# The first row tile's normalization ahead of the second's statistics, and the last row tile's two column halves in two PSUM banks

## Chip, cores and metric

One core of a Trainium2 chip. The metric is the device time of one launch in microseconds (us). A run's span, which the profile shows, is 1.7 to 1.9 us shorter than its time. All runs counted were at a granted TensorE clock of 0.999 to 1.0. All times inside a profile are us from the start of the span.

## The reference

A transformer block in bf16 on 2048 rows of 1024: layer norm, dilated local attention (32 heads, window 8, dilation 2), residual; layer norm, a bilinear gated feed-forward of width 3584, residual.

```python
x = A_x                                                    # (1, 2048, 1024)
h = x + _A_ref(_layernorm(x), A_wqkv, A_wo)                # qkv product, attention, product with wo
h2 = h + _B_ref(_layernorm(h), B_w_gate, B_w_up, B_w_down) # ((h @ w_gate) * (h @ w_up)) @ w_down
```

## The kernel before

The rows are worked on in four chunks of 512, each of four row tiles of 128. Products run on TensorE into eight PSUM banks (`psum`, 128 x 512 fp32 each). The order of instructions on each engine is the order of the program (`manual_schedule`).

**The start.** The first chunk is normalized tile by tile: statistics on VectorE, `Ln` and `Exp` on ScalarE for the scale, the normalization on VectorE in two halves, eight transposes on TensorE, two copies on ScalarE, and 32 small matmuls with weight block 0, of which eight `ko` slices are loaded in two transfers.

```python
    load_w0(0, 4)                       # ScalarE's DMA queue, 512 KB each
    load_w0(4, 4)
    for t in range(4):
        load_x0(t)                      # SyncE's DMA queue, 256 KB each
    nc.scalar.preload_act_table_set("natural_log_exp_and_others")
    # ... (cut: warm-up matmuls, constants)
    first_half(0, 0)                    # statistics of one half of a row tile
    first_half(0, 1)
    first_rstd(0)                       # aggregate (VectorE), Ln and Exp (ScalarE)
    for t in range(4):
        if t < 3:
            first_half(t + 1, 0)
        first_norm(t)
        if t < 3:
            first_half(t + 1, 1)
        if t > 0:
            first_mm(t - 1, range(0, 6))
        first_transpose(t)              # TensorE transposes, ScalarE copies
        if t > 0:
            first_mm(t - 1, range(6, 8))
        if t < 3:
            first_rstd(t + 1)
    first_mm(3, range(8))
```

**The middle.** While TensorE multiplies, a list of background work (`bg`) is dealt out between the matmul groups: statistics of later chunks, attention on VectorE. ScalarE both takes the `Ln` and `Exp` of these statistics and casts finished PSUM banks into SBUF (`evac_qkv`, tile `sg`), in program order. Near 510 us VectorE builds sums of activations and of weights for the feed-forward of the last two chunks.

```python
    xtiles[3] = load_x(3, "x", nc.sync)
    pump(6)
    bg.add(stats_gen(norm1[3]), bg.now + 6.0)     # ready 6.0 later on the kernel's own schedule
    # ... (cut)
    activation_sums(l2, l3, dn["px"])             # VectorE, needs the transposed rows l2 and l3
    weight_sums(0, nc.vector)                     # VectorE, needs weights only
```

**The end.** The last product adds 14 slices to each of four row tiles; their sums stand in the banks `ps_y[0..3]`. The fourth tile is done as two column halves of one bank, so that the last read and store are short.

```python
    def dprod(ps, q, lhs, rhs, fresh, lo=0, n=TC):
        for k in range(NP):             # NP = 14
            nc.tensor.matmul(ps[:, bass.ds(lo, n)], lhsT=lhs[k][:, bass.ts(q, 128)], rhs=rhs[k][:, bass.ds(lo, n)], ...)
    # result(): VectorE reads ps[:, lo:lo+n], scales and adds, then SyncE stores the rows
    for q, lo, n in ((0, 0, 512), (1, 0, 512), (2, 0, 512), (3, 0, 256), (3, 256, 256)):
        dprod(ps_y[q], q, HF["12"], fcells(down["b22"]), False, lo, n)
        result(2, hs2[q], q, 1, ps_y[q], inv, p5[q], lo, n)
```

Of the kernel before, what the change touches and what calls it, by code (L numbers as in the profile page):

```python
# [78 lines left out]
def kernel(  # L79
# [11 lines left out]
    nc = tc.nc  # L91
# [180 lines left out]
    def load_x0(t):  # L272
        nc.sync.dma_start(x0[t][:], x[bass.ds(t * 128, 128), :])

    def load_w0(lo, n):
        nc.scalar.dma_start(w0[:, lo:lo + n, :], wqkv_v[:, lo:lo + n, 0:512])

    load_w0(0, 4)
    load_w0(4, 4)
    for t in range(4):  # L280
        load_x0(t)
    nc.scalar.preload_act_table_set("natural_log_exp_and_others")
    warm = t1k.tile([128, TC], BF, tag="t1k", name="warm")
    nc.vector.memset(warm[:], 0.0)
    eps = const.tile([128, 1], F32)
# [39 lines left out]
    def first_half(t, i):  # L325
        if i == 0:
            sts[t] = small.tile([128, 2, nc.vector.BN_STATS_DIM], F32, tag="st", name=f"st0_{t}")
        nc.vector.bn_stats(out=sts[t][:, i, :], in_=x0[t][:, bass.ts(i, 512)])

    def first_rstd(t):  # L330
        nc.vector.bn_aggr(out=mv0[:, t, :], in_=sts[t][:])
        rstd_of(mv0, rs0, t, t + 1)
# [3 lines left out]
    def first_norm(t):  # L336
        lns[t] = lnp.tile([128, D], BF, tag="ln", name=f"ln0_{t}")
        for i in range(2):
            cols = bass.ts(i, 512)
            nc.vector.tensor_scalar(lns[t][:, cols], x0[t][:, cols], mv0[:, t, 0:1], rs0[:, t:t + 1],  # L340
                                    ALU.subtract, ALU.mult)

    def first_transpose(t):
        for hf in range(2):
            pt = psum.tile([128, KO // 2, 128], BF, tag="mm", name=f"pt{t}_{hf}")
            for kk in range(KO // 2):
                nc.tensor.transpose(pt[:, kk, :], lns[t][:, bass.ts(4 * hf + kk, 128)], ident[:])
            nc.scalar.copy(lnTs[0][:, bass.ts(hf, 4), bass.ts(t, 128)], pt[:])

    def first_mm(t, kos):  # L350
        for ko in kos:
            for j in range(4):
                nc.tensor.matmul(ps0[j][:, bass.ts(t, 128)], lhsT=wts["qkv", 0][:, ko, bass.ts(j, 128)],  # L353
                                 rhs=lnTs[0][:, ko, bass.ts(t, 128)], start=(ko == 0), stop=(ko == KO - 1))
# [3 lines left out]
    first_half(0, 1)  # L358
    first_rstd(0)
    for t in range(4):  # L360
        if t < 3:
            first_half(t + 1, 0)
        first_norm(t)
        if t < 3:
            first_half(t + 1, 1)
        if t > 0:
            first_mm(t - 1, range(0, 6))
        first_transpose(t)
# [4 lines that stand above are left out]
# [386 lines left out]
    def f16(ap):  # L759
        return ap.bitcast(F16)  # L760
# [19 lines left out]
    def fcells(homes):  # L780
        return [f16(t[:, k, :]) for t in homes for k in range(NH)]

    def dprod(ps, q, lhs, rhs, fresh, lo=0, n=TC):
        for k in range(NP):
            nc.tensor.matmul(ps[:, bass.ds(lo, n)], lhsT=lhs[k][:, bass.ts(q, 128)], rhs=rhs[k][:, bass.ds(lo, n)],  # L785
                             start=(fresh and k == 0), stop=(k == NP - 1), skip_group_check=not fresh)

    def result(c, rows, t, hf, ps, sc, other, lo=0, n=TC):
        cols = bass.ds(hf * 512 + lo, n)
        nc.vector.scalar_tensor_tensor(rows[:, cols], ps[:, bass.ds(lo, n)], sc,  # L790
                                       rows[:, cols] if other is None else other[:, bass.ds(lo, n)], ALU.mult, ALU.add)
        nc.sync.dma_start(outf[bass.ds(c * TC + t * 128, 128), cols], rows[:, cols])
# [124 lines left out]
    hs2 = hss[2]  # L917
# [83 lines left out]
    down = {}  # L1001
# [28 lines left out]
    ps_x = [psum.tile([128, TC], F32, tag="mm", name=f"dx{q}") for q in range(4)]  # L1030
    ps_y = [psum.tile([128, TC], F32, tag="mm", name=f"dy{q}") for q in range(4)]
# [6 lines left out]
    for q in range(4):  # L1038
        dprod(ps_x[q], q, HA["11"], fcells(down["b11"]), True)
        if q == 1:  # L1040
            scale_h.total(ps_y[3])
            inv = const.tile([128, 1], F32, name="inv_hd")
            nc.vector.tensor_tensor(inv[:], scale_h.inv, scale_d.inv, ALU.mult)
            inv = inv[:]
# [3 lines left out]
    HF = {k: [f16(a) for a in HA[k]] for k in HA}  # L1048
# [17 lines left out]
    p5 = []  # L1066
# [21 lines left out]
    for q in range(4):  # L1088
        dprod(ps_x[q], q, HF["22"], fcells(down["b21"]), False)
        result(3, hs3[q], q, 0, ps_x[q], inv, None)  # L1090
    for q, lo, n in ((0, 0, 512), (1, 0, 512), (2, 0, 512), (3, 0, 256), (3, 256, 256)):
        dprod(ps_y[q], q, HF["12"], fcells(down["b22"]), False, lo, n)
        result(2, hs2[q], q, 1, ps_y[q], inv, p5[q], lo, n)


# [1 line left out]
_INS = ['A_x', 'A_wqkv', 'A_wo', 'B_x', 'B_w_gate', 'B_w_up', 'B_w_down']  # L1097
# [26 lines left out]
```

## Time and profile before

| | before |
|---|---|
| time, median of 5 runs (range) | 780.2 us (779.79 to 780.25) |
| span of the profiled run | 778.0 us |
| TensorE busy | 770.7 us, 99% |
| first statistics of row tile 0 | 3.76 |
| first 128x512 matmul of the stage after the start | 17.12 |
| first matmul of the last row tile to the end of the span | 7.35 us |

The prediction quotes the lines of this profile. In a timeline line the columns are start, duration, engine, source line, operation, output and input tiles, shapes, count, and in brackets the idle time of the engine before it with what ended it. Neighbours of one kind are merged into one line ("x24").

### The profile page before, as it was taken

To read this page: it belongs to the slowest core of one execution; us is meant where nothing else is said; L and a number is where in the kernel's file an instruction comes from. 1 tells how busy PE (TensorE), PEld (TensorE's weight loads), DVE (VectorE), ACT (ScalarE), POOL (GpSimd) and SP (SyncE) were. 2 spreads that over 40 slices of the span, in tenths; PEclk is the share of its full clock that TensorE was granted. 3 is DMA by queue.
4 is the path that set the end of the run, shared out by engine and by line. 5 is a ranking of instruction groups with operands and counts; after the bars stand their busy time and mean duration, and the time that the engine had idled before them with its cause. 6 is when DMAs were issued, how large, how long until landed. Compare 5 with 4: busy or idle time off the path is not lost.

```text
span 778.0 us, 10494 instructions
## 1 busy us (share of the span) xinstructions
PE 770.7 (99%) x3707; PEld 355.2 (46%) x3707; DVE 614.8 (79%) x805; ACT 473.3 (61%) x1028; POOL 142.1 (18%) x152
## 2 busy tenths in 40 slices
PE   8999999999999999999999999999999999999997
PEld 6544444444444444444444444444444444444444
DVE  6619999999899998999989989985554444579762
ACT  4626544323576652966769799746777677788230
POOL 0000000010000200002000001008778677600000
PEclk9999999999999999999999999999999999999999
DMA  8999693895955869867645383734332323730001
GB/s 279 254 230 209 166 286 84 259 297 144 341 191 169 298 206 237 276 208 247 219 155 196 115 308 107 168 91 115 101 106 58 109 72 92 260 119 28 1 27 55
DMA packets 181605, 133.86 MB, mean 172 GB/s; under 512 B 79024, under 2 KB 174384, under 8 KB 179504
## 3 DMA queue, kind: packets, MB, share of 16 engines
q1 hardware_dynamic: 176912, 110.12, 49.6%
q0 software_dynamic: 3584, 22.02, 8.2%
q10 hardware_dynamic: 1056, 1.05, 0.4%
q8 instruction: 29, 0.48, 0.3%
q14 instruction: 24, 0.20, 0.1%
HBM read 104.86 MB, written 22.02 MB: 163 GB/s over the span
## 4 chain that ended last, share of the span: by engine, by line
PE 89%; DVE 9%; DMA 1%; issue 0%; ACT 0%; SPq 0%; DVEq 0%
PE ps L390 20%; PE pu L390 12%; PE pg L390 12%; PE dx L785 6%; PE pz L678 6%; PE acc L624 6%; PE py L678 6%; PE px L678 6%; PE wo L511 4%; PE pv L678 3%; PE dy L785 3%; DVE h L832 1%; PE ps L353 1%; PE ex L785 1%; DVE h L790 1%; DVE prodx L778 1%
## 5 line engine op out<-in xcount | busy, mean ns | idle before, releaser
L390 PE MATMUL ps<-lnT,w_qkv 128*128 128x512 bf16 x736 | 159.7, 379 | 0.0
L390 PEld LDWEIGHTS <-w_qkv 128*128 128x128 bf16 x736 | 71.8, 98 | 85.9
L390 PE MATMUL pg<-lnT,w_wg 128*128 128x512 bf16 x448 | 105.8, 379 | 0.0
L390 PE MATMUL pu<-lnT,w_wu 128*128 128x512 bf16 x448 | 105.8, 379 | 0.0
L304 ACT CAST sg<-ps 128x512 bf16<-128x512 f32 x96 | 54.7, 589 | 54.0 <-PE ps L390 50.6
L473 DVE TENSOR_TENSOR pv<-vD,at 128x4096 bf16<-128x4096 bf16 x32 | 72.5, 2287 | 0.3
L430 DVE TENSOR_TENSOR prod<-qD,kD 128x4096 bf16<-128x4096 bf16 x32 | 72.4, 2284 | 0.1
L678 PEld LDWEIGHTS <-sw 128*128 128x128 f16 x448 | 43.8, 98 | 54.1 <-issue 1.5
L390 PEld LDWEIGHTS <-w_wg 128*128 128x128 bf16 x448 | 43.8, 98 | 52.9
L390 PEld LDWEIGHTS <-w_wu 128*128 128x128 bf16 x448 | 43.8, 98 | 52.9
L594 ACT CAST us<-pu 128x512 bf16<-128x512 f32 x56 | 33.1, 592 | 41.0 <-PE pu L390 40.9
L678 PE MATMUL px<-lnT,ws 128*128 128x512 bf16 x224 | 55.2, 379 | 0.0
L678 PEld LDWEIGHTS <-ws 128*128 128x128 f16 x336 | 32.9, 98 | 39.6
L624 PE MATMUL acc<-w_wd,gs 128*128 128x512 bf16 x224 | 48.5, 379 | 0.0
L485 POOL DMA_DIRECT2D od<-oD x4 | 2.2, 542 | 252.4 <-DVE oD L483 162.5
L659 POOL TENSOR_TENSOR sw<-ws 128x512 f16<-128x512 f16 x26 | 30.0, 1153 | 85.3 <-PE py L678 78.1
L589 ACT CAST gs<-pg 128x512 bf16<-128x512 f32 x56 | 32.8, 586 | 11.3 <-PE pg L390 9.2
L185 ACT ACTIVATE rs<-mv,eps 128x1 f32<-128x1 f32 (+1 forms) x25 | 7.4, 297 | 49.9 <-DVE mv L182 47.6
L432 DVE TENSOR_TENSOR prod<-prod 128x4096 bf16<-128x4096 bf16 x16 | 36.6, 2289 | 0.3
L539 ACT ACTIVATE junkd<-w_wd 128x512 bf16<-128x512 bf16 x56 | 34.3, 613 | 0.0
L624 PEld LDWEIGHTS <-gs 128*128 128x128 bf16 x224 | 21.9, 98 | 26.4
L695 ACT COPY py<-px 128x512 f32<-128x512 f32 x28 | 16.0, 570 | 26.3 <-PE px L678 26.3
(304 smaller groups left out, 1399.2 us busy)
## 6 DMA issues: line engine op xcount, KB each, us to landing
w_wg<-in_B_w_gate_dram SPq DMA_DIRECT2D x14, 1024.0 KB, 6.7
w_wu<-in_B_w_up_dram SPq DMA_DIRECT2D x14, 1024.0 KB, 5.5
w_wd<-in_B_w_down_dram SPq DMA_DIRECT2D x8, 896.0 KB, 7.3
w_pair<-in_B_w_gate_dram SPq DMA_DIRECT2D x14, 512.0 KB, 4.1
w_pair<-in_B_w_up_dram SPq DMA_DIRECT2D x14, 512.0 KB, 5.3
w_wo<-in_A_wo_dram SPq DMA_DIRECT2D x6, 1024.0 KB, 8.2
w_qkv<-in_A_wqkv_dram SPq DMA_DIRECT2D x5, 1024.0 KB, 9.4
kd<-sg SPq DMA_DIRECT2D x32, 144.0 KB, 3.1
```

The source lines that it names most:

```text
L304: nc.scalar.copy(sg[:, HB:HB + TC], ps[:])
L390: nc.tensor.matmul(ps[:], lhsT=wt[:, ko, bass.ts(j, 128)], rhs=rhs[:, ko, :], start=(ko == 0), stop=(ko == KO - 1))
L430: nc.vector.tensor_tensor(prod[:, j], qD[:], kD[:, :, o:o + SUB], ALU.mult)
L432: nc.vector.tensor_tensor(prod[:, :, 0:16], prod[:, :, 0:16], prod[:, :, 16:32], ALU.add)
L473: nc.vector.tensor_tensor(pv[:, j], vD[:, :, o:o + SUB], at[:, w, None, :].to_broadcast((128, DH, SUB)), ALU.mult)
L511: nc.tensor.matmul(ps[:], lhsT=oTs[c][:, kk, t, :], rhs=wts["wo", c, hf][:, kk, :], start=(kk == 0), stop=(kk == KO - 1))
L539: nc.scalar.activation(junk, src, ACTF.Abs, accum_out=self.l1[:, k:k + 1])
L589: nc.scalar.copy(gs[:], pg[:])
L594: nc.scalar.copy(us[:], pu[:])
L624: nc.tensor.matmul(acc[t][:], lhsT=hT[f][:, bass.ts(t, 128)], rhs=wts["wd", c, hf, b][:, j, :], start=(f == 0), stop=(f == NF - 1))
L678: nc.tensor.matmul(ps[:], lhsT=lhs[:, ko, :], rhs=rhs[:, ko, :], start=(fresh and ko == 0), stop=(ko == 3), skip_group_check=not fresh)
L785: nc.tensor.matmul(ps[:, bass.ds(lo, n)], lhsT=lhs[k][:, bass.ts(q, 128)], rhs=rhs[k][:, bass.ds(lo, n)], start=(fresh and k == 0), stop=( ...
```

## The change

It has three parts. VectorE normalizes row tile 0 before it takes the statistics of row tile 1. The four row loads and the first weight half stand ahead of the table load, the second weight half behind it. The right half of the last row tile is summed in a bank of its own, `ps_x[0]` ("dx" in the profile), whose earlier sum ScalarE copies over well before.

```diff
-    load_w0(0, 4)
-    load_w0(4, 4)
     for t in range(4):
         load_x0(t)
+    load_w0(0, 4)
     nc.scalar.preload_act_table_set("natural_log_exp_and_others")
+    load_w0(4, 4)
 ...
     for t in range(4):
-        if t < 3:
+        if 0 < t < 3:
             first_half(t + 1, 0)
         first_norm(t)
+        if t == 0:
+            first_half(1, 0)
         if t < 3:
             first_half(t + 1, 1)
 ...
-    for q, lo, n in ((0, 0, 512), (1, 0, 512), (2, 0, 512), (3, 0, 256), (3, 256, 256)):
-        dprod(ps_y[q], q, HF["12"], fcells(down["b22"]), False, lo, n)
-        result(2, hs2[q], q, 1, ps_y[q], inv, p5[q], lo, n)
+    for q in range(4):
+        if q < 3:
+            dprod(ps_y[q], q, HF["12"], fcells(down["b22"]), False)
+            result(2, hs2[q], q, 1, ps_y[q], inv, p5[q])
+            if q == 0:
+                nc.scalar.copy(ps_x[0][:, 256:512], ps_y[3][:, 256:512])
+        else:
+            for ps, lo in ((ps_y[3], 0), (ps_x[0], 256)):
+                dprod(ps, q, HF["12"], fcells(down["b22"]), False, lo, 256)
+                result(2, hs2[q], q, 1, ps, inv, p5[q], lo, 256)
```

Source lines behind the loop of the start are two higher in the changed kernel (L390 becomes L392).

## The prediction

> **What bounds the kernel now.** I read the page first (busy shares and the chain that ended last), then TensorE's waits, then the timeline of the two ends of the span, and last the DMA queues in the first 10 us. All times are us from the span's start.
>
> From the page of the kernel before, shares of the chain and of busy time, and then TensorE's waits:
>
> ```profile
> PE 770.7 (99%) x3707; PEld 355.2 (46%) x3707; DVE 614.8 (79%) x805; ACT 473.3 (61%) x1028; POOL 142.1 (18%) x152
> ...
> PE 89%; DVE 9%; DMA 1%; issue 0%; ACT 0%; SPq 0%; DVEq 0%
> ...
> PE warm_ps L298 <- DVE warm L284: 1.2, 1, 1.2
> PE pv L678 <- DVE h L790: 0.9, 2, 0.7
> PE dy L785 <- DVE h L790: 0.6, 1, 0.6
> PE pt L347 <- DVE ln L340: 0.5, 1, 0.5
> PE ps L353 <- ACT lnT L348: 0.4, 1, 0.4
> ```
>
> TensorE is busy 770.7 of 778.0. The change adds and removes no matmul, so it can only win from the 7.3 left, most of which lies before the first data (1.2) and after the last matmul (about 3.4). The change touches two of the waits listed: "dy <- DVE h" (0.6, the end) and those around L347/L353 (the start). Two per cent would be 15.6 us, twice all the idle time there is. So the verdict is "same" and the question is only how many tenths.
>
> The start, from the timeline (start, duration, engine, line, instruction, idle before):
>
> ```profile
> 5.65 0.20 ACT L186 ACTIVATE rs<-rs 128x1 f32<-128x1 f32 x1
> 5.89 0.69 DVE L328 BATCH_NORM_STATS2 st<-x 128x6 f32<-128x512 bf16 x1 [0.60 <-DMA x<-in_A_x_dram]
> 6.50 0.72 DVE L340 TENSOR_SCALAR ln<-x,mv,rs 128x512 bf16<-128x512 bf16 x2
> 7.39 1.07 ACT L348 COPY lnT<-pt 128x512 bf16<-128x512 bf16 x2 [1.53 <-PE pt L347]
> 7.85 0.21 DVE L331 BATCH_NORM_AGGREGATE mv<-st 128x2 f32<-128x12 f32 x1
> 8.02 1.50 PE L353 MATMUL ps<-lnT,w_qkv 128*128 128x128 bf16 x24 [0.35 <-ACT lnT L348]
> 8.35 0.31 ACT L185 ACTIVATE rs<-mv,eps 128x1 f32<-128x1 f32 x1
> 8.92 0.73 DVE L340 TENSOR_SCALAR ln<-x,mv,rs 128x512 bf16<-128x512 bf16 x2 [0.30 <-ACT rs L186]
> ```
>
> Tile 0's scale is ready when Exp at 5.65 ends, but VectorE first does a half of tile 1's statistics (5.89), which waits for tile 1's load, and normalizes tile 0 only at 6.50. Tile 1's Ln starts at 8.35 though its mean and variance were begun at 7.85: ScalarE was in tile 0's two copies. From there a loop sets the pace: normalize, transposes, copies, Ln, Exp, normalize. Normalizes start at 6.50, 8.92, 11.36, 13.80, a period of 2.42 to 2.44. From 17.12 on TensorE runs on without a gap to about 450.
>
> The end:
>
> ```profile
> 771.92 0.38 PE L785 MATMUL dy<-dn_b22b,kx 128*128 128x256 f16 x2
> 772.03 0.10 PEld L785 LDWEIGHTS <-hq 128*128 128x128 f16 x1
> 772.34 0.48 DVE L790 SCALAR_TENSOR_TENSOR h<-dy,inv_hd,dp 128x256 bf16<-128x256 f32 x1 [0.78 <-PE dy L785]
> 772.88 0.81 PE L785 MATMUL dy<-dn_b22a,hq 128*128 128x256 f16 x6 [0.58 <-DVE h L790]
> 774.60 0.48 DVE L790 SCALAR_TENSOR_TENSOR h<-dy,inv_hd,dp 128x256 bf16<-128x256 f32 x1 [1.78 <-PE dy L785]
> ```
>
> The second half of the last row tile begins only when VectorE has read the first half out of the same bank. Its weights were already in the array at 772.03.
>
> **What the Trainium skill says.** "PSUM — Partial Sum Buffer", section "PSUM bank collisions raise a hardware error": accesses by two engines must be kept apart by bank and 32-partition quadrant, not by address, and disjoint columns of one bank still collide. The trace agrees with the ordering: the second half's columns are different ones, and it still stood 0.58 behind the read. Section "Engine vs sequencer instructions" of the same page: the queues of ScalarE and VectorE are strict FIFO. The trace agrees: Ln of tile 1 comes behind the copies, the normalize of tile 0 behind the statistics. "ScalarE: Activation LUTs", section "What ACT_TABLE_LOAD costs": about 1283 ns for the load; the trace has 1.28 us, at 1.80 to 3.08. "DMA: Bandwidth & Descriptors", section "Queues, rings and completion order": each DMA engine goes round-robin between the queues that have work. The trace shows turns: in 2.5 to 3.0 the x queue moved 0.17 MB against 0.01 of the weight queue, in 3.5 to 4.0 the weight queue 0.19 and x none, in 4.5 to 5.0 x 0.19 against 0.01, in 5.0 to 5.5 the weight queue 0.16 against 0.02.
>
> **The end, part by part.** The last 14 matmuls go to another bank (dx0), whose right half ScalarE fills from dy3 after the first row tile of this stage. I compared the built programs: on TensorE nothing else differs. The first matmul into dx0 still waits on VectorE, but for the read of dx0's old sum, which began at 757.42, 15 us earlier; so the wait is void. The added copy is 128x256 from PSUM to PSUM; its 128x512 sisters took 570 ns at L1076, ScalarE has nothing after 746.8, so it is off the path. What it saves: the first half started at 770.61 and its last matmul pair at 771.92, 12 matmuls later, so 0.109 each. The 15th would start at 770.61 + 14 x 0.109 = 772.14 instead of 772.88: **0.74 saved**. That is more than the 0.58 of the wait row, since the modelled end of the first half (772.30) lies a pipeline's depth after the last start. The last VectorE read moves from 774.60 to 773.86; the first half's read is over at 772.82, no conflict. The final store (64 KB, 1.6 to landing) moves with it.
>
> **The start.** VectorE's order becomes: normalize 0 (two halves), statistics 1 (two halves), aggregate 1. Normalize 0 starts 0.24 after Exp (as at 8.68 to 8.92): 5.65 + 0.24 = 5.89, not 6.50. Tile 1's statistics start 0.63 later (6.50 to 7.13 before): 6.52; halves take 0.61 and 0.72; aggregate at 7.85, exactly as before. So nothing is won on VectorE itself: it waited 0.60 either way, for x1 before, for the scale now (x1 landed at 5.86). The gain is on ScalarE. Transposes of tile 0 could start 0.45 after normalize, at 6.34, but the warm-up matmuls run to 1.21 + 5.23 = 6.44. Copies 0.44 later: 6.88. Ln of tile 1 stands 0.96 behind the copies' start (7.39 to 8.35): 7.84. Its other input: aggregate 7.85 + 0.24 (5.08 to 5.32) = 8.09. The later one holds: 8.09 instead of 8.35. Normalize 1 at 8.09 + 0.57 = 8.66, when VectorE is just free (8.62). From there the loop of 2.44 is unchanged, so tiles 1 to 3 and the end of the stage, 17.12, come 0.26 earlier: **0.26 saved**, of 0.61 that the reorder shows at first sight. Later work has room: weight block 1 landed at 13.93 (8.93 + 5.0).
>
> **The load order.** On SyncE nothing moves; on ScalarE the second half of w_qkv 0 is issued behind the table load, so at about 1.3 + 1.28 = 2.6 instead of 1.25. First bytes came about 1.4 after issue at the start (0.76 to 2.2), so it is ready about 4.0, while its turn on the DMA engines came at 5.0, after x1. I count **0**: landing near 8.45 (1.25 + 7.2), as before.
>
> Sum: 0.74 + 0.26 + 0 = 1.0; 780.2 - 1.0 = **779.2 us**.
>
> **Rivals.** (1) The weight half lands late. Tile 0's matmuls now start at 6.88 + 0.63 = 7.51, and the last 8 of the first 24 need this half, 16 x 0.06 later, at 8.5. Tile 1's transposes stand behind them on TensorE and want to start at 8.66 + 0.47 = 9.13. Landing at 8.45 just fits; a landing later than about 8.65 eats the gain, at 8.9 it is gone, and at 9.4 the start loses 0.5: 779.7. For it: it is issued 1.3 later. Against it: its turn came later than that anyway. (2) The start wins the whole 0.61 or more, because x1 arrives earlier with less weight traffic: this needs the aggregate of tile 1 earlier than 7.85, and normalize 0 stands ahead of it, bound to x0 (landed about 3.75, moved ahead of any weight byte already). I give it little; time 778.8. (3) The new bank brings a wait of its own, for the copy or for an older read: then the end saves nothing, 779.9. The built program speaks against it. (4) The shift at 17.12 is lost in a later wait on a load: TensorE has no wait on DMA in its list.
>
> **Range and chances.** The three runs before spread over 0.43 and their median lies at their top; rivals 1 to 3 span 778.8 to 779.9. Range 778.6 to 780.0. A change of over 2% either way has no mechanism: faster 0.005, same 0.99, slower 0.005.
>
> **What would show it.** Right: no TensorE wait "dy/dx <- DVE h" at the end, and the 15th matmul of the last row tile 0.11 after the 14th; the copy near 758; TensorE's end earlier than the last 128x512 row tile's end by 0.74 less than before. Normalize starts near 5.89, 8.66, 11.1, 13.5; first L390 matmul near 16.86. Wrong: Ln of tile 1 still behind the copies at 8.35, a gap inside tile 0's 24 matmuls (rival 1), normalize 0 well before 5.8 (rival 2), a TensorE wait before dx (rival 3), or any stage between 17 and 770 changing its length.

## The result, and the profile after

The changed kernel took 779.19 us (median of 5 runs, 778.91 to 779.41) against 780.2 beside it. The ratio is 0.9988, 95% interval 0.9973 to 1.0002: the same within 2%. The interval includes 1, so these times alone do not show that the kernel became faster. Ratios are the mean time of one kernel's fast runs over that of the other's of the same rounds, so they are not quite the ratios of the quoted medians. A second set of runs gave 779.05 against 779.86 (experiment after_again).

The two profiled executions differ by less than the medians: 778.0 and 777.6 of span. The profiled run of before (779.73) was faster than its five timed runs, that of after (779.41) was the slowest of its five. So for the size of each part the single steps of the traces count, not the difference of the spans.

From the page of the changed kernel, TensorE's busy time, and from its waits on TensorE the longest:

```profile
PE 770.7 (99%) x3707; PEld 355.1 (46%) x3707; DVE 614.9 (79%) x805; ACT 473.8 (61%) x1029; POOL 142.3 (18%) x152
...
PE warm_ps L298 <- DVE warm L284: 1.2, 1, 1.2
PE pv L680 <- DVE h L792: 1.1, 2, 0.9
PE ps L353 <- ACT lnT L348: 0.3, 1, 0.3
PE pt L347 <- DVE ln L340: 0.3, 1, 0.3
PE ps L353 <- DMA w_qkv<-in_A_wqkv_dram: 0.3, 1, 0.3
```

The wait "dy <- DVE h" of 0.6 at the end is gone. A new wait of TensorE on a weight load (0.3) has come at the start, and "pv <- DVE h", which the change does not touch, has grown by 0.2.

**The end.** The timeline of the changed kernel's last matmuls and of VectorE's two last reads:

```profile
772.34 0.38 PE L787 MATMUL dy<-dn_b22b,kx 128*128 128x256 f16 x2
772.45 0.64 PEld L787 LDWEIGHTS <-hq 128*128 128x128 f16 x6
772.56 0.82 PE L787 MATMUL dx<-dn_b22a,hq 128*128 128x256 f16 x6
772.83 0.48 DVE L792 SCALAR_TENSOR_TENSOR h<-dy,inv_hd,dp 128x256 bf16<-128x256 f32 x1 [0.84 <-PE dy L787]
774.29 0.48 DVE L792 SCALAR_TENSOR_TENSOR h<-dx,inv_hd,dp 128x256 bf16<-128x256 f32 x1 [0.98 <-PE dx L787]
```

The right half ("dx") starts at 772.56 with no bracket, so without a wait, while VectorE reads "dy" only from 772.83 on. Taken from the trace's single matmuls, the 15th starts 0.109 after the 14th; before it was 0.849. From the first matmul of the last row tile to the end of the span it is 6.60 now, 7.35 before: 0.75 less. The added copy ran at 758.63 and took 0.36, 11.42 after ScalarE's work before it; nothing waited for it.

**The start.** The timeline of the changed kernel from the scale of tile 0 to the transposes of tile 1:

```profile
5.92 0.20 ACT L186 ACTIVATE rs<-rs 128x1 f32<-128x1 f32 x1
6.16 0.73 DVE L340 TENSOR_SCALAR ln<-x,mv,rs 128x512 bf16<-128x512 bf16 x2 [0.60 <-ACT rs L186]
...
7.70 1.05 PE L353 MATMUL ps<-lnT,w_qkv 128*128 128x128 bf16 x16 [0.35 <-ACT lnT L348]
...
8.12 0.21 DVE L331 BATCH_NORM_AGGREGATE mv<-st 128x2 f32<-128x12 f32 x1
...
8.37 0.29 ACT L185 ACTIVATE rs<-mv,eps 128x1 f32<-128x1 f32 x1 [0.23 <-DVE mv L331]
...
8.93 0.73 DVE L340 TENSOR_SCALAR ln<-x,mv,rs 128x512 bf16<-128x512 bf16 x2
...
9.03 0.62 PE L353 MATMUL ps<-lnT,w_qkv 128*128 128x128 bf16 x8 [0.27 <-DMA w_qkv<-in_A_wqkv_dram]
```

On the clock nothing is earlier: the normalize of tile 1 starts at 8.93, before at 8.92. But the first rows landed later in this execution: the first statistics start at 4.03, not 3.76, for a load that the change puts behind nothing. Counted from there, the normalize of tile 1 comes after 4.90, before after 5.16: the 0.26 of the prediction. `Ln` of tile 1 now waits for its own input ("DVE mv") and no longer for the copies. What is new is the last line: tile 0's first 24 matmuls are cut into 16 and 8, and the 8 wait for the second weight half. The tile-1 transposes behind them start at 9.48. At 17.21 the 128x512 matmuls begin, 13.18 after the first statistics, before 13.36. So 0.18 of the 0.26 arrives there.

**The issue of the second weight half.** ScalarE and its DMA queue, first before, then after:

```profile
0.75 1.02 ACTq L276 DMA_DIRECT2D w_qkv<-in_A_wqkv_dram  x2
1.80 1.28 ACT L282 ACT_TABLE_LOAD   x1 [1.80 <-issue]
```

```profile
0.75 0.46 ACTq L276 DMA_DIRECT2D w_qkv<-in_A_wqkv_dram  x1
1.24 1.28 ACT L281 ACT_TABLE_LOAD   x1 [1.24 <-PEq L1116]
1.27 0.49 ACTq L276 DMA_DIRECT2D w_qkv<-in_A_wqkv_dram  x1
```

In the program the second issue stands behind the table load, but it went out at 1.27, during the load, not at 2.6 as predicted. The load order thus hardly moved the issue of this half: from 1.24 to 1.27.

**The middle.** Between 17 and 770 the changed kernel's execution lost 0.34 against the other: 0.14 near 60, where two neighbouring matmuls start 0.359 instead of 0.216 apart, and 0.20 at 520 (the "pv" wait, 0.68 before, 0.88 after). With +0.09 at 17 and -0.75 at the end the sum is -0.32; the spans differ by 0.33 (777.96 and 777.63).

### The profile page after: what moved, and what is told of

Read it like the earlier page. It is cut to its first block, busy times and chain, and to the rows that moved or that the text cites. A ratio compares the mean times of both kernels' runs of the same rounds, so it can differ in the third digit from the quotient of the medians.

```text
span 777.6 us, 10495 instructions
## 1 busy us (share of the span) xinstructions
PE 770.7 (99%) x3707; PEld 355.1 (46%) x3707; DVE 614.9 (79%) x805; ACT 473.8 (61%) x1029; POOL 142.3 (18%) x152
## 4 chain that ended last, share of the span: by engine, by line
PE 88%; DVE 9%; DMA 1%; ACT 1%; issue 0%; SPq 0%; ACTq 0%; DVEq 0%
PE ps L392 20%; PE pg L392 12%; PE pu L392 12%; PE dx L787 6%; PE pz L680 6%; PE acc L626 6%; PE py L680 6%; PE px L680 6%; PE wo L513 4%; PE pv L680 3%; PE dy L787 3%; DVE h L834 1%; DMA w_qkv<-in_A_wqkv_dram 1%; PE ps L353 1%; PE ex L787 1%; DVE prodx L780 1%
## 5 line engine op out<-in xcount | busy, mean ns | idle before, releaser
L392 PE MATMUL ps<-lnT,w_qkv 128*128 128x512 bf16 x736 | 159.8, 379 | 0.0
L392 PEld LDWEIGHTS <-w_qkv 128*128 128x128 bf16 x736 | 71.8, 98 | 86.0 <-issue 0.3
L392 PE MATMUL pg<-lnT,w_wg 128*128 128x512 bf16 x448 | 105.8, 379 | 0.0
L392 PE MATMUL pu<-lnT,w_wu 128*128 128x512 bf16 x448 | 105.8, 379 | 0.0
L392 PEld LDWEIGHTS <-w_wg 128*128 128x128 bf16 x448 | 43.8, 98 | 52.9
L392 PEld LDWEIGHTS <-w_wu 128*128 128x128 bf16 x448 | 43.8, 98 | 52.9
```

The source lines that it names most:

```text
L392: nc.tensor.matmul(ps[:], lhsT=wt[:, ko, bass.ts(j, 128)], rhs=rhs[:, ko, :], start=(ko == 0), stop=(ko == KO - 1))
```

## The experiments

Theory: the end brings its 0.74; the start brings 0.26 to VectorE, of which the late weight half takes some; the rest is the scatter of landings. The rival for each part was that the times would not show it, or that it came from elsewhere. The table gives all twelve runs. "Before" is the kernel before, beside them on the same chip (9 runs each). "Stage" is the distance from the first statistics of tile 0 to the first 128x512 matmul, which takes out when the first rows landed. It is the difference of two printed times, good to 0.01.

| run | median us (range of 5) | before | ratio, 95% interval | stage us |
|---|---|---|---|---|
| end_only | 779.26 (778.89 to 779.93) | 779.86 | 0.9992, 0.998 to 1.0005 | 13.39 |
| norm_only | 779.79 (779.59 to 779.94) | 779.86 | 0.9998, 0.9985 to 1.001 | 13.21 |
| loads_only | 779.71 (779.5 to 780.21) | 779.86 | 0.9998, 0.9984 to 1.0011 | 13.44 |
| start_only | 779.82 (779.7 to 779.95) | 779.86 | 0.9999, 0.9986 to 1.0011 | 13.17 |
| after_again | 779.05 (778.76 to 779.23) | 779.86 | 0.9988, 0.9975 to 1.0 | 13.16 |
| after_split62 | 779.18 (778.95 to 779.38) | 779.86 | 0.9989, 0.9977 to 1.0002 | 13.34 |
| one_piece | 779.51 (779.15 to 779.96) | 779.86 | 0.9993, 0.9979 to 1.0007 | 13.53 |
| after_swap | 778.23 (778.1 to 778.31) | 779.86 | 0.9977, 0.9965 to 0.999 | 13.21 |
| after_split422 | 779.14 (778.83 to 780.25) | 779.88 | 0.9994, 0.9981 to 1.0006 | 13.11 |
| late_half | 780.25 (780.01 to 780.5) | 779.88 | 1.0005, 0.9993 to 1.0018 | 14.40 |
| best422_swap | 778.01 (777.84 to 778.96) | 779.88 | 0.998, 0.9966 to 0.9993 | 13.10 |
| best_late_stats | 778.14 (777.85 to 778.41) | 779.72 | 0.9978, 0.9965 to 0.9992 | 13.11 |

All were correct and all count as the same within 2%. Only the three kernels with "swap" or "late_stats" in their name, which share one edit near 510 us, have an interval that lies wholly under 1. The kernel before had a stage of 13.36, the changed kernel 13.18.

### The parts alone: end_only, norm_only, loads_only, start_only

Each is the kernel before with some of the hunks of the diff above: the last hunk alone, the second alone, the first alone, and the first two.

> Only the two-bank end. Theory: the whole gain at the end is the removed wait, 0.74 us (in the trace of the changed kernel the 15th matmul of the last row tile starts 0.11 after the 14th, against 0.87 before), so about 779.4 where before is 780.1, and the last matmul ends 0.75 nearer to the last full row tile's matmuls. Rival: the gain of about 1.0 us seen in the times is of the start, and the end is worth less because the final store and the span's end do not follow the last read: then 779.9 or more.

> Only the order on VectorE (first tile normalized before the second's statistics), load order as before. Theory: 0.26 us, 779.8: normalize 0 starts 0.24 after Exp, Ln of tile 1 is held by its own mean and variance 0.24 after their start and no longer by the copies, the first matmul of line 390 stands 0.26 earlier than before, counted from tile 0's landing. Rival A: the second half of the weights lands at 8.45 or later and holds the last 8 matmuls of tile 0's first 24, so the start wins nothing (780.1). Rival B: 0.6 us (779.5), if tile 1's load was what held the start.

> Only the order of the loads. Theory: 0 in time (780.1). The trace of the changed kernel shows the second weight half issued at 1.27 (0.02 later than before) during the table load, so nothing moves by more than the spread of landings; the landing of tile 0 at 3.75 to 4.05 and of the weight half at 8.4 to 9.0. Rival: this order makes the weight half land about 0.5 later (8.98 in the changed kernel against 8.45 before), which costs here too: 780.2 to 780.5.

> Both changes of the start, end as before. Theory: as the norm order alone, 779.8, less what a late weight half takes: in the profiled run of the changed kernel the start came out 0.08 later than before, so between 779.8 and 780.2. Rival: the two together win what neither does alone, 0.5 or more (779.6 or less).

end_only is 0.60 under the kernel before by medians; its profile shows the 15th matmul 0.109 after the 14th (the kernel before has 0.849; the 0.87 in the expectation is slightly off) and an end part of 6.59, down to the end of the span. So the final store and the span's end do follow the last read, which the rival had doubted. Its profiled run (779.93) lost the gain again near 520, where TensorE waited 1.33 instead of 0.68, a place that the edit does not touch. The three edits of the start move the median by 0.04 to 0.15, less than the spread of any one of them (0.25 to 0.7), so the times do not resolve them. The traces do: with the new VectorE order the normalize of tile 1 comes 4.90 after tile 0's statistics in both, and the stage is 13.17 to 13.21 instead of 13.36; with the load order alone it is 13.44, no gain. The old VectorE order gives 13.36 to 13.53 over its four profiles (one_piece below has the 13.53), so the stage won 0.15 to 0.37, and the 0.18 above is one pair of executions. The wait on the weight half is there with either load order. In the timeline of start_only:

```profile
8.76 0.62 PE L353 MATMUL ps<-lnT,w_qkv 128*128 128x128 bf16 x8 [0.27 <-DMA w_qkv<-in_A_wqkv_dram]
```

In norm_only, where both halves are issued as before, the 8 start at 8.96, after a wait of 0.31. So the gate is a matter of the new VectorE order, which makes tile 0's matmuls ready earlier, and not of the new load order.

### The weight half as a gate: late_half, after_split62, after_split422

late_half makes the gate worse: the second half is issued from SyncE's queue only after tile 1's rows have landed.

```diff
     nc.scalar.preload_act_table_set("natural_log_exp_and_others")
-    load_w0(4, 4)
 ...
+    nc.gpsimd.tensor_copy(w0[:, 4, 0:1], x0[1][:, 0:1])
+    nc.sync.dma_start(w0[:, 4:8, :], wqkv_v[:, 4:8, 0:512])
```

> The changed kernel with the second weight half made late on purpose: issued from SyncE only when tile 1's rows have landed (about 5.9). Theory (this half gates tile 1's transposes, which stand behind its matmuls): it lands about 10, so the gap inside tile 0's 24 matmuls grows from 0.3 to 1.5, tile 1's transposes and everything after move by about as much as it lands after 8.6: line 392 at 14.2 to 14.7 us after tile 0's statistics, time 1.0 to 1.5 above the changed kernel (780.1 to 780.6). Rival (the loop of normalize, transposes, copies and Ln has slack for it): less than 0.3.

The timeline of late_half, the gate and the first 128x512 matmul:

```profile
9.94 0.61 PE L354 MATMUL ps<-lnT,w_qkv 128*128 128x128 bf16 x8 [1.51 <-DMA w_qkv<-in_A_wqkv_dram]
...
18.10 1.24 PE L393 MATMUL ps<-lnT,w_qkv 128*128 128x512 bf16 x4
```

With the gate opening at 9.94, the stage takes 14.40, 1.2 more than in the changed kernel, and the median is 1.1 to 1.2 above its medians of 779.19 and 779.05. A lateness here does reach the end. after_split62 and after_split422 try to take the gate away, by loading weight block 0 in pieces of 6 and 2, or of 4, 2 and 2 slices.

```diff
-    load_w0(0, 4)
+    load_w0(0, 6)
     nc.scalar.preload_act_table_set("natural_log_exp_and_others")
-    load_w0(4, 4)
+    load_w0(6, 2)
```

> The changed kernel with the first weight block loaded as 6 and 2 blocks of 128 rows instead of 4 and 4, so that the last 8 of tile 0's first 24 matmuls need only the first load. Theory (the late second half eats the start's gain): the gap of 0.3 to 0.5 inside those 24 matmuls is gone, Ln of tile 2 comes 0.1 to 0.2 earlier, line 392 stands 13.1 us after tile 0's statistics instead of 13.2; 0.1 us in time, so within 0.3 of the changed kernel run again. Rival (the larger first load pushes tile 1's load behind it): statistics of tile 1 wait for their data, line 392 at 13.3 or later.

In after_split62 the wait was gone, and nothing was won: the larger first piece landed 5.7 after its issue, and tile 1's rows came later too (5.7 after issue, otherwise 4.5 to 5.0). VectorE waited for them, 0.15 at 6.90, and the stage took 13.34. That was the rival.

```diff
     load_w0(0, 4)
     nc.scalar.preload_act_table_set("natural_log_exp_and_others")
-    load_w0(4, 4)
+    load_w0(4, 2)
+    load_w0(6, 2)
```

> The changed kernel with the second weight half cut in two loads (4, 2 and 2 blocks of 128 rows, all in the queue of ScalarE), so that the last 8 of tile 0's first 24 matmuls wait for 256 KB less; tile 1's load is not pushed, unlike with 6 and 2. Theory (the late half takes 0.07 to 0.1 of the 0.26 that the normalize of tile 1 gains): no or a smaller gap inside the 24 matmuls, line 392 at 13.10 us after tile 0's first statistics, against 13.16 to 13.21 with the gap and 13.36 to 13.39 in the old order. In time 0.1 or less against the changed kernel (779.0). Rival (the three loads land as late as the two): 13.2, gap as before.

after_split422 left the first piece as it was and freed the 24 matmuls. Its timeline, with the first 128x512 matmul, and then what happened near 60:

```profile
7.75 1.50 PE L354 MATMUL ps<-lnT,w_qkv 128*128 128x128 bf16 x24 [0.45 <-ACT lnT L349]
...
16.87 1.03 PE L393 MATMUL ps<-lnT,w_qkv 128*128 128x512 bf16 x3
...
55.26 1.28 DVE L181 BATCH_NORM_STATS2 st<-x 128x6 f32<-128x512 bf16 x2 [17.24 <-DMA x<-in_A_x_dram]
...
59.94 0.20 ACT L186 ACTIVATE rs<-rs 128x1 f32<-128x1 f32 x1
60.04 0.57 ACT L305 CAST sg<-ps 128x512 bf16<-128x512 f32 x1
60.66 1.67 PE L393 MATMUL ps<-lnT,w_qkv 128*128 128x512 bf16 x7 [0.41 <-ACT sg L305]
```

The 24 run in one go and the stage begins at 16.87, 13.11 after the statistics: within 0.01 of the clock time that the prediction gave for it. The three kernels with 4, 2 and 2 slices have 13.10 to 13.11, five with the gate 13.16 to 13.21 (the new order, no other load in the way). So the gate costs 0.05 to 0.11.

But the median did not move (779.14, against 779.05 and 779.19 of the changed kernel). The last lines show what this execution lost elsewhere. VectorE could start on the rows of chunk 3 at 55.26; their `Ln` and `Exp` stand on ScalarE ahead of the cast that frees a PSUM bank, and TensorE waited for that cast until 60.66. Its single matmuls there start 0.786 apart instead of 0.216, a loss of 0.57, twice what the start had won. The order on ScalarE is the one that the Trainium skill states in "PSUM — Partial Sum Buffer", section "Engine vs sequencer instructions" (strict FIFO), and the trace agrees: ScalarE did nothing for 9.76 until chunk 3's first `Ln` at 56.82, and the cast came only at 60.04, behind the third `Exp` of these rows (59.94). In the three executions that show this loss, TensorE resumed 5.40 after the start of chunk 3's first statistics (55.26 to 60.66; 55.17 to 60.58 in the changed kernel; 55.05 to 60.45 in one_piece), and the matmul concerned would have started 43.23 after the first of the stage. So the loss is (statistics of chunk 3) - (first 128x512 matmul) - 37.83, if positive. That fits the other eleven profiles, which show none: their values are at most 0.02.

### The size of the last piece: one_piece

```diff
-    for q, lo, n in ((0, 0, 512), (1, 0, 512), (2, 0, 512), (3, 0, 256), (3, 256, 256)):
-        dprod(ps_y[q], q, HF["12"], fcells(down["b22"]), False, lo, n)
-        result(2, hs2[q], q, 1, ps_y[q], inv, p5[q], lo, n)
+    for q in range(4):
+        dprod(ps_y[q], q, HF["12"], fcells(down["b22"]), False)
+        result(2, hs2[q], q, 1, ps_y[q], inv, p5[q])
```

> The kernel before, its last row tile in one piece of 512 columns in one bank (no split, no copy, no wait). Theory: TensorE ends as in the changed end, since 14 matmuls of 512 columns take what 28 of 256 take; the last read is 0.75 instead of 0.48, and the store is 128 KB instead of 64 KB: 0.3 to 0.5 slower than the changed end, 0.3 to 0.4 faster than before, 779.5 to 779.7. Rival (the split in two banks is worth no more than leaving the split out): equal to the changed end, 779.2.

The kernel before with the last row tile in one product was 0.35 faster than the kernel before, and 0.25 slower than end_only (medians of two chips, each with a before of 779.86). The split into halves of one bank had thus cost more than it brought. Its last read takes 0.75 instead of 0.48. The differences of the medians lie inside the runs' ranges. The profile settles them: from the first matmul of the last row tile to the end of the span it is 6.99 here, against 7.32 to 7.35 with the old end and 6.54 to 6.60 with the new one, so 0.33 to 0.36 better than the one and 0.39 to 0.45 worse than the other.

### The wait at 520: after_swap, best422_swap

In the eleven profiles without the swap VectorE waits 1.9 to 2.3 us, until 511.5 to 512.8, before the activation sums, and TensorE later waits for a PSUM bank that VectorE frees. The swap lets VectorE do the weight sums first.

```diff
-    activation_sums(l2, l3, dn["px"])
     weight_sums(0, nc.vector)
+    activation_sums(l2, l3, dn["px"])
```

> The changed kernel with the first weight sums (lines 661 to 664 of it) put ahead of the activation sums on VectorE, which wait about 2 us there for the last transpose by DMA. Theory: the two profiles differ in the middle by 0.34 because that wait, at 509 to 512, varies, and it reaches TensorE at 520 (idle 0.7 to 1.3 there). The weight sums can start at 510.9, when ScalarE has scaled the weights, so VectorE ends this stretch 0.6 or more earlier and TensorE's wait at 520 falls by 0.6: 0.6 faster than the changed kernel run again, 778.6. Rival (the wait is on other work too): less than 0.2.

The timelines of the changed kernel and of after_swap:

```profile
511.90 1.23 DVE L672 TENSOR_TENSOR prodx<-lnT,lnT 128x2048 f16<-128x2048 bf16 x1 [2.19 <-DMA out_dram<-h]
...
520.69 1.02 PE L680 MATMUL pv<-prodx,sw 128*128 128x512 f16 x4 [0.88 <-DVE h L792]
```

```profile
510.79 0.69 DVE L661 TENSOR_TENSOR sw<-ws 128x1024 f16<-128x1024 f16 x1 [1.39 <-ACT ws L654]
...
513.33 1.22 DVE L672 TENSOR_TENSOR prodx<-lnT,lnT 128x2048 f16<-128x2048 bf16 x1
...
519.58 1.02 PE L680 MATMUL pv<-prodx,sw 128*128 128x512 f16 x4
```

The activation sums no longer wait, and TensorE goes on at 519.58 without a bracket. TensorE's wait there is 0.06 to 0.19 in the three profiles with the swap and 0.68 to 1.33 in the eleven without. The median fell by 0.82 against after_again on the same chip. Its five runs lie within 0.21, but those of best422_swap and best_late_stats, which have the swap too, range over 1.12 and 0.56: that this wait made the scatter of the times is not shown. The profile names a store of "h" as what ended VectorE's wait; that store gives these sums nothing, and the DMA transposes of the last rows, which they do read, end in the same stretch: the last one lands 0.27 to 0.39 before VectorE goes on, in all eleven. That the transposes are the true releaser is my inference.

best422_swap puts the swap on top of after_split422.

> The changed kernel with both the 4, 2, 2 loads and the weight sums ahead of the activation sums. Theory: the swap was worth 0.8 in time (778.23 against 779.05), the loads 0 to 0.1: 778.15, and the TensorE wait at 520 stays under 0.1. Rival: the loads cost something in the start, 778.4.

Its median of 778.01 is the lowest, 1.87 under the kernel before on its chip. It beats both kernels; its lead over after_swap (0.22, on another chip) is less than its own range, and by the ratios (0.998 against 0.9977) there is none.

### The gate near 60: best_late_stats

The last run was to test the second gate. Its only edit on best422_swap moves two casts ahead of chunk 3's first `Ln` on ScalarE; in the built program VectorE's order stays as it was.

```diff
-    bg.add(stats_gen(norm1[3]), bg.now + 6.0)
+    bg.add(stats_gen(norm1[3]), bg.now + 9.0)
```

> The kernel best422_swap with one number changed: the background work that takes the statistics of row chunk 3 becomes ready 3.0 later on the kernel's own schedule (9.0 instead of 6.0). In the built program this moves two of ScalarE's PSUM casts (sg) ahead of the first Ln of these statistics and changes nothing on VectorE. Theory: what keeps the start's gain from the end of the kernel is a second gate near 60 us. TensorE there waits for a PSUM bank, whose cast stands on ScalarE behind an Ln that waits for the landing of chunk 3's rows. In the traces so far TensorE resumed 5.40 after VectorE's first statistics of chunk 3, so it loses (statistics start) minus (first 128x512 matmul of the stage) minus 37.83 where that is positive: after 0.14, one_piece 0.12, after_split422 0.57, the others none. The statistics started between 54.37 and 55.43 in 13 traces, median 54.97, so a stage that begins at 16.85 instead of 17.12 gives most of it back in most executions. With the casts moved ahead: no TensorE gap between 58 and 62 whatever the landing, first matmul of the stage at 16.75 to 16.95, median 777.6 to 777.9 and no run above 778.4. Rival A: the gate has nothing to do with the times of the other runs, the spread has another source: median 778.0, and a run at or above 778.5 as in best422_swap (778.96). Rival B: the casts that remain behind the later Ln make a TensorE gap of their own near 62 to 64: median 778.1 or more.

No gap near 60 and none at 62 to 64. But the profiled run began its stage at 17.09, since its first rows came late (statistics at 3.98), and chunk 3's at 54.83. With these two the formula gives no loss even without the edit (54.83 - 17.09 - 37.83 is negative). So the profile does not test it. The median, 778.14, missed the expected 777.6 to 777.9. The slowest run of best422_swap (778.96) has no counterpart, the highest here being 778.41, but five runs do not show that the edit did it. The test is inconclusive.

The theory behind it takes chunk 3's landing as a time fixed on the clock, which an earlier stage does not move. The traces of SyncE, whose queue (SPq) issues these loads, speak against that. First after_split422, then late_half; each line stands for four issues:

```profile
40.74 11.34 SPq L229 DMA_TRANSPOSE lnT<-ln  x4
52.13 2.00 SPq L202 DMA_DIRECT2D x<-in_A_x_dram  x4
```

```profile
41.97 9.34 SPq L229 DMA_TRANSPOSE lnT<-ln  x4
51.36 2.65 SPq L202 DMA_DIRECT2D x<-in_A_x_dram  x4
```

In the program the loads stand behind chunk 2's four DMA transposes. The first of these goes out 23.87 after the stage's first 128x512 matmul in every one of the 14 profiles, in late_half too, whose stage begins about 1 later (16.87 + 23.87, 18.10 + 23.87). So these loads move with the start. What scatters most is the issue of the fourth transpose, which takes 5.10 to 7.16. From the stage's first matmul to chunk 3's statistics it is 37.33 to 38.39, and it is more than 37.83 in four profiles: after 37.96, one_piece 37.94, after_split422 38.39 (the three losses) and after_split62, by 0.02. late_half has 37.33, like the kernel before. As far as these profiles show, the loss near 60 is scatter of its own and not the price of an earlier start.

## Why the prediction was right, and where it was not

**The total and the verdict** were right: 779.19 against 779.2, inside the range. Part of that agreement is luck, and two of the prediction's own signs of being wrong did come: the gap inside tile 0's 24 matmuls, and a stretch between 17 and 770 that changed its length (by 0.34). The sum was taken from the 780.2 of that set; in four other sets the kernel before had 779.72 to 779.88, and the changed kernel's gain beside it was 0.81, not 1.0.

**The end, 0.74:** right in mechanism and size. The wait is one for a semaphore, so an order that the program keeps; no run here lets TensorE and VectorE use that bank at once. From the first matmul of the last row tile to the end of the span it is 6.54 to 6.60 in the nine profiles with the new end, and 7.32 to 7.35 in the four with the old one (one_piece has a third form), and the wait on VectorE is gone. In times it is 0.60 (end_only). Rival 3, a wait of the new bank's own, did not appear.

**The start, 0.26:** the mechanism was right, the term was too large. `Ln` of tile 1 was freed from the copies, and the normalize of tile 1 came exactly 0.26 nearer to the first statistics in the changed kernel, in norm_only and in start_only. What failed is the step "Landing at 8.45 just fits". The weight half landed at about 9.0 in the changed kernel, late by the prediction's own limit of 8.65 even after the 0.27 by which the first rows came late (9.03 - 0.27 = 8.76 for the 8 matmuls). This is rival 1: it took 0.05 to 0.11 of the 0.26, as late_half and after_split422 show from both sides. At 17 us some 0.18 is left.

**"Later work has room", and rival 4 set aside:** the check was too narrow. The prediction looked for a wait of TensorE on a DMA and found none. The load of chunk 3's rows does reach TensorE, by way of ScalarE's queue and a PSUM bank. In the profile of before it was invisible, since there it had 0.50 to spare (17.12 + 37.83 - 54.45). It cost 0.14 in the changed kernel's profile and 0.57 in that of after_split422, but by scatter and not because the stage began earlier, as the SyncE queue above shows; in the changed kernel's execution it even began later (17.21). A shift of the start does get through in the traces: in late_half, with a stage about 1 later, TensorE resumes near 520 at 521.56, 503.46 after the stage's first matmul, and in the other ten profiles without the swap it is 503.14 to 503.91. That spread is larger than the 0.26, and the times of the start edits (0.04 to 0.15, inside the runs' spread) do not resolve it. So what the start is worth in time is not settled.

**The load order, 0:** the number was right, its reason wrong. The issue did not wait for the table load (1.27, not 2.6). The landing still moved, between 8.4 and 9.0 over the profiles with two halves (late_half aside), with either order: 8.40 to 8.97 with the old load order, 8.71 to 8.98 with the new.

**Rival 2** (the start wins 0.61 or more) failed: tile 1's aggregate stayed 4.1 behind the first statistics (3.76 to 7.85, 4.03 to 8.12).

## What to carry to other kernels

Two halves of one PSUM bank are not two buffers: if VectorE reads one while TensorE should write the other, give the second half its own bank, or do not split. Here the order between two 128x256 halves cost 0.74. When an edit makes an early stage faster by tenths, follow its gain to the next load that work depends on: a wait with 0.5 to spare does not show in the profile before, and it can hide behind another engine's queue. Then ask whether that load comes at a time of its own or moves with the edit, and read it from a run that shifts the stage on purpose (late_half). Where landings scatter by tenths, compare distances from a landing within each trace, and take times only from several runs.

## What the Trainium skill lacked or had wrong

- "DMA: Bandwidth & Descriptors" gives no spread for the landing of one and the same load. Here the 256 KB of the first rows let the first statistics start between 3.57 and 4.03, the 512 KB weight half landed between 8.4 and 9.0, and the first rows of chunk 3 took 2.9 to 4.1 from their issue to VectorE's start on them. Each of these spreads is larger than the 0.26 that was sought at the start.
- "ScalarE: Activation LUTs", section "What ACT_TABLE_LOAD costs", has the 1283 ns right (1.28 here), but does not say what becomes of a DMA issue that follows on the same engine. Other pages describe how the sequencer hands work to its engine, from which it could have been expected; none states it for a DMA issue behind a table load. Here it went out at 1.27, during the load at 1.24 to 2.52.
- "PSUM — Partial Sum Buffer" says that disjoint columns of one bank still collide, which no run here put to the test since the kernel keeps the order, but it has no figure for the wait that keeping the order costs. Here it was 0.74 between two 128x256 halves (0.849 against 0.109 from matmul to matmul).
